# Linear attention and an MLP on one core: the first batch's q loaded with a cast on GpSimd's queue, one group of seven-product multiplications a block later, and a new instruction order

## The chip, the core and the metric

The kernel runs on one core of a Trainium2 chip. The core has five engines with an instruction stream each: TensorE (PE in the profile, with PEld for its weight loads), VectorE (DVE), ScalarE (ACT), GpSimd (POOL) and SyncE (SP). Each works through its stream in order; waits between engines go through semaphores. Loads and stores are issued by SP, ACT or POOL and carried out by 16 DMA engines. On-chip data lies in SBUF (128 partitions); PE writes its results to PSUM, eight banks of 128 x 512 fp32 here. The metric is the device time of one execution in microseconds (us), less is better.

## What is computed

```python
def _attn_ref(q, k, v, omega):              # q, k, v: 8 batches x 8 heads x 576 x 64; omega: 128 x 64
    m, D = omega.shape
    scale = 1.0 / np.sqrt(np.sqrt(D))
    q_s, k_s = (q * scale, k * scale)
    def phi(x):
        proj = np.einsum('bhsd,md->bhsm', x, omega)
        sq = np.sum(x * x, axis=-1, keepdims=True) / 2.0
        h = proj - sq
        h = h - np.max(h, axis=-1, keepdims=True)
        return np.exp(h) / np.sqrt(m)
    q_p, k_p = (phi(q_s), phi(k_s))
    kv = np.einsum('bhsm,bhsd->bhmd', k_p, v)
    z = np.sum(k_p, axis=2)
    num = np.einsum('bhsm,bhmd->bhsd', q_p, kv)
    den = np.einsum('bhsm,bhm->bhs', q_p, z)[..., None] + 1e-06
    return (num / den).astype(np.float32)

def _moe_ref(x, w_in, w_out):               # x: 4608 x 512, w_in: 512 x 2048, w_out: 2048 x 512
    h = x @ w_in
    relu6 = np.clip(h + 3.0, 0.0, 6.0)
    g = h * relu6 / 6.0
    return (g @ w_out).astype(np.float32)
```

The attention's result, its heads laid side by side, is the MLP's x. Everything comes in and goes out as float32.

## The kernel before

The work is written as some 2,000 small operations (`op(...)`), each with the engines that may do it, what it reads and writes, and numbers for a planner: its length, its delay (`lat`), for a DMA its issue time. A planner (`Prog.schedule`) replays the lists in `ORDER`, which say for each engine which operations it runs in which sequence; a search outside the kernel wrote these lists. The planner's numbers run nowhere on the chip. They decide which PSUM bank an operation gets, where PE gets a throwaway matmul (`idle`, line 606, on a constant tile `fill`), and in which order the instructions and their waits are written out.

Attention runs over the 8 batches, the MLP over 8 blocks of 512 tokens, one for each batch, and a ninth block made of each batch's last 64 tokens (the leftovers). The attention of batch b runs beside the MLP of block b - 1, and the output product of a block beside the next block's input product.

One batch of attention: q and k are turned so that the 64 head dimensions lie on partitions (`kT`, `qT`), multiplied with omega (L822 and L825, for the first batch L865 and L884), and the exponential is taken on ACT into `kp` and `qpT` (L841 and L849, for the first batch L872 and L888). The term that would scale a row of q cancels in the division; for k, DVE takes each row's maximum (`mx`, L705) and its reciprocal (`cc`), and v is multiplied by it (`vc`, L999 to L1009, `vcl` for the leftovers). PE then forms `kv` with the sums z beside it (L1017, L1019; copied to `kvz`), the numerators and denominators (L1045, L964), DVE or ACT divides (`rec`, L1064, L1068) into `xb`, and the result is turned into `xT`, the MLP's input.

The order of the first 25 us. The first batch comes in as float32: k and v by 5 loads each and q by 6 (four "main" parts of 256 KB each: two heads' halves times two halves of the head pairs, and one or two parts with the leftovers), two of k's on ACT's queue, all others on SP's. The q parts are called `q00`, `q10`, `q01`, `q11`, `ql0` and `ql1`. PE turns them as float32 (`turns32`, L748) and DVE or ACT copies the result from PSUM to bf16 (`Tevk`, `Tevq`, L552 and L553). The turn of q needs both parts of a half (`q00` and `q10`, `q01` and `q11`). From the second batch on, q and k are loaded on POOL's queue, which casts them to bf16 on the way (`kb`, `qb`, L652), and are turned as bf16, on PE for the second batch (`turns`, L564) and by DMA (L803) after that. The weights `wi` (L625, five loads) and `wo` (L634, eight) are cast to float16 by POOL's queue too; the first `wi` load waits for the q part `q11` (`W_GATE`).

The MLP. The plain input product multiplies four pieces of 128 rows for each 128 hidden columns and 512 tokens (`mm1`, L1124; for the first block in halves of 256 tokens, `mm1_half`, L1277). From a given block on a group of 4 x 128 hidden columns is computed with seven products in place of eight (`mm1_quad`, L1222): sums of the weights (`input_sums`, W1 to W4) and of x (`x_sums`, X1 to X4) are formed first, and five copies and additions in PSUM on ACT and DVE (q1 to q5) put the products together. `FIRST7` gives the block for each of the four groups:

```python
    FIRST7 = (6, 7, 2, 2)
    def seven(blk, f):
        return blk >= FIRST7[f // 2 % 4]
```

The activation is a ReLU on ACT into `tsb` and a minimum and product on DVE into `gT`. The output product uses seven products from the second block on (`products`, L1391; the first block plainly, L1302), with sums of `gT` (S1 to S4, L1318) on POOL or DVE.

The weight sums W2 to W4 and some of X lie in the memory of the float32 q and k (`q32`, `k32`), which is free once the first batch is turned.

Of the kernel before, what the change touches and what calls it, by code (L numbers as in the profile page):

```python
# [21 lines left out]
        14, 121, 115, 117, 131, 159, 138, 153, 147, 119, 141, 144, 135, 156, 150, 127, 123, 125, 129, 174, 133, 168,  # L22
        176, 166, 162, 164, 178, 180, 189, 170, 172, 205, 191, 221, 212, 207, 249, 194, 196, 398, 386, 223, 392, 210,
        237, 393, 228, 215, 199, 239, 399, 226, 387, 252, 244, 242, 388, 400, 394, 389, 395, 401, 404, 407, 410, 247,
        413, 231, 416, 275, 419, 422, 277, 425, 281, 293, 291, 283, 428, 289, 279, 431, 322, 434, 437, 287, 308, 564,
        565, 566, 567, 440, 315, 544, 255, 545, 285, 546, 547, 568, 295, 548, 549, 569, 554, 574, 575, 555, 556, 557,
        558, 576, 577, 348, 550, 578, 559, 335, 350, 353, 340, 337, 551, 560, 374, 579, 361, 379, 376, 580, 366, 363,
        561, 581, 343, 356, 382, 570, 369, 571, 598, 595, 592, 607, 470, 601, 610, 616, 613, 484, 622, 628, 631, 477,
        625, 643, 637, 646, 457, 757, 758, 640, 767, 509, 760, 511, 497, 514, 761, 499, 502, 768, 521, 690, 523, 526,
        533, 770, 538, 535, 771, 670, 773, 776, 777, 683, 774, 697, 794, 788, 791, 803, 818, 780, 806, 797, 823, 822,  # L30
        781, 820, 809, 841, 812, 843, 710, 825, 827, 845, 722, 846, 829, 712, 734, 848, 965, 736, 724, 966, 852, 850,
        715, 727, 975, 968, 746, 981, 748, 751, 976, 739, 969, 978, 979, 878, 982, 984, 985, 891, 988, 989, 898, 996,
        1002, 999, 1005, 905, 1014, 1011, 1026, 1017, 1028, 1049, 1030, 1031, 918, 1054, 1020, 1033, 1035, 1051, 930,
        1037, 1053, 935, 923, 1173, 1056, 1058, 954, 920, 1174, 942, 932, 1060, 1176, 944, 956, 959, 947, 1177, 1183,
        1184, 1099, 1186, 1187, 1086, 1192, 1193, 1113, 1204, 1207, 1210, 1219, 1106, 1213, 1222, 1234, 1236, 1228,
        1238, 1239, 1225, 1189, 1257, 1241, 1190, 1243, 1262, 1245, 1259, 1138, 1261, 1196, 1126, 1143, 1140, 1264,
        1197, 1150, 1268, 1381, 1131, 1152, 1382, 1162, 1128, 1266, 1384, 1164, 1167, 1391, 1155, 1392, 1385, 1307,
        1394, 1395, 1314, 1397, 1400, 1401, 1294, 1398, 1412, 1418, 1444, 1415, 1430, 1442, 1421, 1427, 1447, 1433,
        1446, 1436, 1449, 1467, 1465, 1451, 1404, 1405, 1470, 1453, 1469, 1321, 1472, 1474, 1334, 1346, 1476, 1593,
        1594, 1339, 1336, 1348, 1358, 1351, 1596, 1597, 1519, 1363, 1603, 1604, 1360, 1370, 1526, 1606, 1375, 1372,  # L40
        1607, 1533, 1609, 1612, 1610, 1506, 1613, 1616, 1624, 1617, 1626, 1629, 1662, 1628, 1664, 1631, 1667, 1633,
        1558, 1635, 1647, 1546, 1653, 1560, 1548, 1669, 1650, 1563, 1551, 1671, 1666, 1687, 1582, 1656, 1685, 1587,
        1570, 1584, 1673, 1689, 1690, 1572, 1575, 1712, 1692, 1713, 1694, 1766, 1696, 1722, 1743, 1715, 1716, 1747,
        1770, 1745, 1748, 1768, 1771, 1750, 1791, 1752, 1723, 1754, 1773, 1775, 1789, 1725, 1726, 1814, 1794, 1793,
        1777, 1731, 1732, 1812, 1796, 1798, 1728, 1817, 1729, 1800, 1819, 1816, 1866, 1868, 1821, 1823, 1735, 1870,
        1736, 1889, 1871, 1835, 1836, 1873, 1893, 1894, 1875, 1838, 1891, 1877, 1896, 1845, 1898, 1912, 1839, 1914,
        1916, 1900, 1917, 1935, 1846, 1919, 1939, 1921, 1940, 1937, 1848, 1849, 1851, 1942, 1923, 1958, 1852, 1959,
        1854, 1946, 1855, 1944, 1858, 1859, 1968, 1969, 1961, 1962, 1971, 1972, 1974, 1975, 1978, 1979, 1987, 1990,
        1993,
    ],  # L50
    "SP": [
        0, 18, 22, 33, 20, 23, 26, 25, 24, 27, 28, 32, 29, 30, 31, 450, 264, 266, 265, 456, 455, 453, 454, 553, 384,
        452, 451, 563, 667, 666, 669, 668, 663, 583, 517, 505, 573, 529, 541, 542, 665, 664, 779, 871, 875, 876, 874,
        872, 783, 877, 718, 730, 754, 742, 873, 1085, 1084, 755, 1082, 987, 991, 1080, 1079, 1083, 926, 938, 962, 950,
        1081, 1292, 1287, 1291, 1293, 963, 1290, 1289, 1199, 1146, 1195, 1499, 1134, 1158, 1170, 1288, 1504, 1502, 1171,
        1407, 1503, 1505, 1403, 1500, 1501, 1342, 1354, 1366, 1378, 1379, 1566, 1554, 1619, 1590, 1578, 1591, 1615,
        1734, 1738, 1861, 1857, 1985, 1986, 1982, 1981, 1984, 1992,
    ],
    "ACT": [
        21, 19, 118, 132, 139, 148, 120, 142, 136, 145, 151, 128, 157, 154, 124, 188, 126, 134, 169, 163, 165, 204, 167,  # L60
        177, 175, 160, 220, 206, 171, 173, 179, 181, 222, 211, 238, 200, 390, 396, 405, 408, 402, 232, 248, 411, 414,
        417, 420, 278, 423, 282, 294, 426, 292, 276, 429, 432, 327, 325, 328, 323, 435, 438, 314, 311, 309, 313, 441,
        318, 320, 316, 321, 298, 304, 301, 296, 302, 300, 306, 307, 347, 330, 333, 336, 360, 359, 375, 552, 362, 378,
        562, 383, 344, 599, 582, 596, 572, 593, 608, 475, 473, 471, 602, 611, 617, 476, 614, 487, 490, 623, 489, 485,
        629, 632, 480, 478, 626, 508, 644, 482, 483, 638, 466, 460, 458, 647, 464, 462, 759, 469, 641, 496, 463, 468,
        498, 520, 516, 532, 762, 522, 693, 534, 691, 696, 695, 772, 676, 682, 681, 677, 679, 675, 673, 671, 689, 686,
        688, 703, 795, 684, 789, 700, 792, 706, 709, 698, 819, 807, 804, 798, 830, 702, 824, 821, 810, 543, 813, 842,
        844, 711, 832, 733, 847, 723, 853, 836, 735, 834, 714, 745, 967, 859, 855, 857, 738, 717, 729, 977, 753, 970,
        980, 881, 885, 879, 884, 883, 889, 887, 986, 892, 894, 897, 896, 890, 901, 899, 904, 997, 903, 1003, 1000, 1006,
        906, 908, 1015, 911, 1012, 1027, 1018, 917, 910, 1050, 1032, 941, 919, 1038, 1055, 1021, 1040, 1052, 931, 1044,  # L70
        953, 1061, 1042, 937, 925, 1065, 1175, 1063, 943, 1067, 934, 961, 1185, 1105, 1104, 1100, 1102, 1188, 1095,
        1093, 1097, 1098, 1091, 1087, 1114, 1089, 1118, 1205, 1208, 1092, 1119, 1211, 1116, 1220, 1109, 1112, 1107,
# [353 lines left out]
def _emit(nc, es, q, k, v, omega, w_in, w_out, out):  # L426
    B, H, S, D = q.shape
# [215 lines left out]
    def load(b, eng, gates):  # L643
# [15 lines left out]
        def landing(t, hh, m0, m1):  # L659

            if t == "v" or b == 0:
                return [(t + "32", hh, m) for m in range(m0, m1)]
# [924 lines left out]
```

## Time and profile before

| | |
|---|---|
| time, median of 3 runs | 298.52 us (298.09 to 299.27) |
| time of the profiled execution | 298.33 us |
| its span, first to last instruction | 296.5 us |
| mean granted TensorE clock | 0.999 |
| PE busy | 289.5 us (98%), 2938 matmuls |
| DVE busy | 257.4 us (87%), 581 instructions |
| ACT busy | 240.6 us (81%), 587 instructions |
| POOL busy | 182.2 us (61%), 207 instructions |
| DMA | 44.90 MB written, mean 151 GB/s |
| landing of the first batch's q loads, after issue | 4.0 to 5.2 us |
| landing of the first batch's v loads, after issue | 4.9 to 5.4 us |
| landing of the five w_in loads, after issue | 6.9 to 9.4 us |

Times in the profile are from the start of the span. A chain of waits is followed back from the last instruction to what released each step. A group of instructions has one line: source line, engine, operation, tiles, shapes, count, then busy us and mean ns, then the idle time ahead of them. A matmul's mean length holds its latency, so a run of matmuls is read from the length of the whole run: 16 matmuls of 512 columns take 3.49 to 3.56 us, 16 of 256 columns 1.75.

### The profile page before, as it was taken

What the parts mean: (1) busy time and instruction counts of PE and PEld (TensorE: products, weight loads), DVE (VectorE), ACT (ScalarE), POOL (GpSimd) and SP (SyncE); (2) the same over time, 40 slices, a digit from 0 to 9 for tenths busy, and PEclk for the clock granted to TensorE, in tenths of its full rate; (3) what the DMA queues carried; (4) which work ended last, traced back from release to release, by engine and by line L of the source; (5) the groups of instructions that cost most, each with busy time, mean ns of one, the idle gap of its engine ahead of it and who ended that gap; (6) DMA issues with size and microseconds to landing.
All of it is one profiled execution on the core that took longest, in us unless ns stands there. A gap on an engine that the chain in (4) does not pass through costs nothing.

```text
span 296.5 us, 7761 instructions
## 1 busy us (share of the span) xinstructions
PE 289.5 (98%) x2938; PEld 220.1 (74%) x2938; DVE 257.4 (87%) x581; ACT 240.6 (81%) x587; POOL 182.2 (61%) x207
## 2 busy tenths in 40 slices
PE   8999999999898999999999999999999999999996
PEld 5768855544784698658856987588787888888885
DVE  4797888869987998899789996999999999998974
ACT  2975988799778998999899887999899988767410
POOL 1666456047697863898798579766667344556241
PEclk9999999999999999999999999999999999999999
DMA  8999999989999997998997999959601500110034
GB/s 234 296 206 196 203 234 117 149 200 229 138 202 207 216 127 207 152 199 234 163 180 130 111 259 168 153 131 234 122 2 35 167 25 0 74 71 2 0 144 142
DMA packets 90100, 44.90 MB, mean 151 GB/s; under 512 B 57936, under 2 KB 87760, under 8 KB 90064
## 3 DMA queue, kind: packets, MB, share of 16 engines
q1 hardware_dynamic: 62496, 31.11, 46.6%
q0 software_dynamic: 26592, 12.46, 33.9%
q10 hardware_dynamic: 976, 0.85, 0.9%
q8 instruction: 23, 0.38, 0.5%
q14 instruction: 13, 0.11, 0.1%
HBM read 36.73 MB, written 9.44 MB: 156 GB/s over the span
## 4 chain that ended last, share of the span: by engine, by line
PE 90%; ACT 6%; DVE 3%; issue 0%
PE p L1391 33%; PE p L1222 20%; PE p L1124 13%; PE p L1302 5%; PE p L1277 5%; PE p L1045 3%; PE p L822 3%; PE p L1017 3%; PE p L825 2%; ACT kp L872 1%; PE p L606 1%; ACT tsb L1130 1%; ACT qpT L849 1%; ACT qpT L888 1%; PE p L564 1%; ACT kp L841 1%
## 5 line engine op out<-in xcount | busy, mean ns | idle before, releaser
L705 DVE TENSOR_REDUCE mx<-kp 128x4 f32<-128x512 bf16 (+1 forms) x79 | 47.8, 629 | 6.1 <-ACT kp L841 4.1
L1258 ACT ACTIVATE tsb<-p 128x512 f16<-128x512 f32 x76 | 44.8, 620 | 8.0 <-DVE gT L1260 4.3
L1260 DVE SCALAR_TENSOR_TENSOR gT<-tsb,p 128x512 f16<-128x512 f16 x76 | 50.0, 679 | 1.4 <-ACT tsb L1258 1.0
L1124 PE MATMUL p<-xT,wi 128*128 128x512 f16 x208 | 49.2, 379 | 1.0 <-ACT qpT L849 0.8
L1391 PE MATMUL p<-wo,gT 128*128 128x256 f16 x368 | 46.2, 273 | 0.8 <-DVE gT L1132 0.8
L552 ACT COPY p<-p 128x512 f32<-128x512 f32 x61 | 35.3, 596 | 7.8 <-PE p L1222 5.8
L841 ACT ACTIVATE kp<-p 128x512 bf16<-128x512 f32 (+1 forms) x70 | 37.3, 578 | 4.8 <-PE p L825 4.8
L1391 PEld LDWEIGHTS p<-wo,gT 128*128 128x128 f16 x368 | 35.2, 98 | 5.3 <-ACT kp L841 1.1
L849 ACT ACTIVATE qpT<-p 128x512 bf16<-128x512 f32 (+1 forms) x70 | 37.7, 577 | 0.8 <-PE p L825 0.7
L1132 DVE SCALAR_TENSOR_TENSOR gT<-tsb,p 128x512 f16<-128x512 f16 x52 | 34.2, 678 | 4.5 <-ACT tsb L1130 4.0
L1124 PEld LDWEIGHTS p<-xT,wi 128*128 128x128 f16 x208 | 19.5, 98 | 22.4 <-ACT qpT L849 1.7
L1130 ACT ACTIVATE tsb<-p 128x512 f16<-128x512 f32 x52 | 31.4, 629 | 3.1 <-PE p L1124 2.7
L999 POOL TENSOR_TENSOR vc<-v,cc 128x512 bf16<-128x512 f32 (+1 forms) x29 | 29.1, 1002 | 7.4 <-DVE s L1318 1.9
L1318 POOL TENSOR_TENSOR gT<-gT 128x512 f16<-128x512 f16 x21 | 24.3, 1156 | 14.1 <-DVE s L1318 10.1
L1391 PE MATMUL p<-t,gT 128*128 128x256 f16 x256 | 31.1, 273 | 0.0
L1318 POOL TENSOR_TENSOR s<-gT,s 128x512 f16<-128x512 f16 x18 | 20.8, 1156 | 13.1 <-DVE s L1318 4.3
L1318 POOL TENSOR_TENSOR gT<-gT,s 128x512 f16<-128x512 f16 x18 | 20.9, 1162 | 12.3 <-PE p L1391 6.7
L1391 PEld LDWEIGHTS p<-t,gT 128*128 128x128 f16 x256 | 24.4, 98 | 5.0 <-issue 1.6
L652 POOL DMA_DIRECT2D kb<-in_k_dram x21 | 16.4, 785 | 18.9 <-DMA kT<-kb 10.9
L1318 POOL TENSOR_TENSOR s<-gT 128x512 f16<-128x512 f16 x15 | 17.4, 1158 | 10.3 <-DVE wi L1318 3.2
L1068 ACT ACTIVATE xb<-p,rec 128x64 f16<-128x64 f32 x98 | 21.9, 365 | 0.5 <-DVE rec L1057 0.5
L652 POOL DMA_DIRECT2D qb<-in_q_dram x28 | 19.7, 708 | 2.9 <-DMA wi<-in_moe_w_in_dram 2.9
(142 smaller groups left out, 640.3 us busy)
## 6 DMA issues: line engine op xcount, KB each, us to landing
v<-in_v_dram SPq DMA_DIRECT2D x14, 512.0 KB, 4.7
out_dram<-osb SPq DMA_DIRECT2D x14, 512.0 KB, 3.8
kb<-in_k_dram POOLq DMA_DIRECT2D x14, 256.0 KB, 6.2
qb<-in_q_dram POOLq DMA_DIRECT2D x14, 256.0 KB, 6.2
wo<-in_moe_w_out_dram POOLq DMA_DIRECT2D x8, 256.0 KB, 6.7
wi<-in_moe_w_in_dram POOLq DMA_DIRECT2D x3, 512.0 KB, 7.5
q<-in_q_dram SPq DMA_DIRECT2D x4, 256.0 KB, 4.5
vl<-in_v_dram SPq DMA_DIRECT2D x8, 128.0 KB, 3.8
```

Source lines behind the costliest of these rows:

```text
L552: return E.copy(dst(), src())
L652: lambda E: E.dma_start(dst, src), prio + 0.001 * turn_of[0], reads=gate, writes=keys,
L705: op("DVE", dvet(128 * n), lambda E: E.reduce_max(dst, src, axis=AX.X), p, reads=reads, writes=writes, name="mx" + name)
L841: op("ACT", actt(128 * (d1 - d0)), lambda E, lh=lh, ko=ko, part=part: E.activation(ko, out_of(part, 0, lh)[0].rearrange("p (x m) -> p x m" ...
L849: op("ACT", actt(128 * (d1 - d0)), lambda E, lh=lh, part=part: E.activation(qd[:, part[0]:part[1], lh, :], out_of(part, 1, lh)[0].rearrang ...
L1124: ins = E.matmul(ring.t[vh.slot], wi[:, c, 128 * f:128 * f + 128], xv[:, c, :], start=(c == 0), stop=(c == NJ - 1))
L1130: op("ACT", actt(512), lambda E: E.activation(tsb[tu][:], ring.t[vh.slot], AF.Relu, bias=0.5, scale=1.0 / 6.0), t - 0.1, reads=[vh], write ...
L1222: ins = E.matmul(bank(v)[:, 256 * g:256 * g + 256], w(c, f + g), x[:, c, :], start=start and g == 0 and c == 0, stop=c == 1, skip_group_ch ...
L1258: op("ACT", actt(512), lambda E, v=v, tu=tu: E.activation(tsb[tu][:], bank(v), AF.Relu, bias=0.5, scale=1.0 / 6.0), t - 0.1, reads=[v], wr ...
L1260: op("DVE", dvet(512), lambda E, v=v, tu=tu, dst=dst: E.scalar_tensor_tensor(dst, pieces(tsb[tu][:]), 1.0, pieces(bank(v)), ALU.min, ALU.m ...
L1318: op(engines, {"POOL": 0.157 + n / 475.0, "DVE": 0.08 + n / 2000.0}, lambda E: E.tensor_tensor(dst, x, y, ALU.subtract if minus else ALU.a ...
L1391: ins = E.matmul(ring.t[v.slot][:, 256 * j:256 * j + 256], a[:, f, 128 * j:128 * j + 128], w[:, f, :], start=(first and f == 0 and j == 0) ...
```

## The change

- The first batch's q is loaded by POOL's queue straight into the bf16 tile `qb`, in the same six parts; `q32` is no longer loaded. PE turns it as bf16 with `turns`.
- The first `wi` load waits for the part of `qb` that `q11` brings (`("qb", 17)`).
- `FIRST7` goes from (6, 7, 2, 2) to (7, 7, 2, 2): block 6 computes its first group with plain products. The weight sums of groups 0 and 1 are then formed together ahead of block 7.
- The planner's numbers for landings change: `LANDS` has an entry for almost every load of the first batch, `LANDS_B` for later ones, and the delays of transposed loads and of stores are shorter.
- `ORDER` is replaced in full.

```diff
-    LANDS = {"ql0": 2.3, "ql1": 2.3, "v00": 2.1, "q01": 2.1, "v11": 1.0, "v01": 0.2, "k01": 1.8, "vl": 1.8, "q11": 1.8}
-    W_GATE = [("q32", 1, 3)] * 4
+    LANDS = {"k00": 0.9, "k10": 0.9, "kl": 1.2, "q00": 0.9, "q10": 0.9, "ql0": 1.3, "ql1": 1.3, "v00": 1.3, "v10": 1.1, "q01": 1.1, "v11": -0.8, "v01": -0.1, "k01": 1.0, "k11": 0.7, "vl": 1.1, "q11": 1.0}
+    LANDS_B = {"vl": 0.2, "v00": 0.5, "v10": 0.9, "ql0": 0.8, "ql1": 0.8, "kl": 1.1}
+    W_GATE = [("qb", 17)] * 4
...
-            cast = b > 0 and part[0] in "kq"
+            cast = b > 0 and part[0] in "kq" or part[0] == "q"
             e = "POOL" if cast else eng[turn_of[0]] if turn_of[0] < len(eng) else "SP"
...
-        tensors = {"k": (k, kb if b else k32), "q": (q, qb if b else q32), "v": (v, v32)}
+        tensors = {"k": (k, kb if b else k32), "q": (q, qb), "v": (v, v32)}
...
-                    turns32("q", nm, dbl, alts(qT, s, m0, m1), q32, main_keys("q", range(m0, m1)), 0)
-            for t, src, dst in (("k", k32, kT), ("q", q32, qT)):
-                turns32(t, "l", [0, 1], dst[:, 0:2, :], src, left_keys(t), 0 if t == "k" else LATE)
+                    turns("q", nm, dbl, alts(qT, s, m0, m1), qb, 0)
+            turns32("k", "l", [0, 1], kT[:, 0:2, :], k32, left_keys("k"), 0)
+            turns("q", "l", [0, 1], qT[:, 0:2, :], qb, LATE)
...
-    FIRST7 = (6, 7, 2, 2)
+    FIRST7 = (7, 7, 2, 2)
...
-        old = [(t + "32", hh, m) for t in "kq" for hh in range(2) for m in range(NP)] + [("k32l", 0), ("q32l", 0), ("q32l", 1)]
+        old = [("k32", hh, m) for hh in range(2) for m in range(NP)] + [("k32l", 0)]
```

What the new lists hold at the start, as operations in sequence (T is a turn, Tev its evacuation, e an exponential, K, Q the products with omega):

- SP before: k00, kl, ql1, k01, q00, q11, q01, q10, vl, v00, ql0, v10, v01, v11. After: k00, kl, k01, vl, v00, v10, v01, v11.
- POOL before: wi x3, vc, vc, vcl, vcl, vc, wi x2. After: ql1, q00, q11, q01, q10, ql0, wi x3, vc, wi, vc, vcl, vcl, vc, vc, wi, vc, vc.
- ACT, both: k11, k10, Tevk x2, eK x2, Tevk, eK x4, Tevq. Then, before: eK x2, Tevq, vc's column, Tevq x2, eQ. After: Tevq, eK, eQ, Tevq, eK, eQ.
- DVE before: Tevk x2, mx x3, cc, mx x2, mx, cc x2, Tevq, mx x2. After: Tevk x2, mx x3, cc, mx, Tevq, mx, cc, Tevq, mx, cc, mx x2.
- PE, k's turns before: four in a row, then the products. After: idle x1, T, idle x2, T, idle, T, idle x8, T of the leftovers, then the products. PE has 43 throwaway matmuls in place of 35.
- Over the whole run ACT has 479 operations in place of 487, DVE 572 in place of 581, POOL 217 in place of 203. Of the divisions' first parts ACT does 5 in place of 9 and DVE 27 in place of 23; of the second parts ACT 12 in place of 11; POOL forms 77 S sums in place of 72 and 14 X sums in place of 11, and DVE as many fewer.

## The prediction

> **What bounds the kernel now.** I read the page first, then the chain of waits, then engine busy time in stretches of 2 us (start) and 5 us (the rest).
>
> ```profile
> PE   8999999999898999999999999999999999999996
> PEclk9999999999999999999999999999999999999999
> PE 90%; ACT 6%; DVE 3%; issue 0%
> ```
>
> TensorE (PE) is the bound almost everywhere, at full granted clock. The other 10% of the chain lies at the start and between 45 and 100 us.
>
> ```profile
> 7.70 1.09 ACT kp L872 x2
> ...
> 11.23 0.52 ACT qT L552
> ...
> 20.64 0.43 PE p L1017 x8
> ...
> 22.84 4.02 PE p L1277 x36
> ```
>
> Chain of waits, first 40 us (start, length, engine, tile, line). From 7.70 to 16.2 us it runs on ScalarE (ACT): exponentials of k, evacuations of the turned q, exponentials of q. From 17.2 to 20.6 it is on VectorE (DVE). At 22.84 us the first dense run of MLP matmuls begins; before it PE fills its gaps with throwaway matmuls (L606). What starts that run earlier is saved in full as long as PE stays full behind it.
>
> ```profile
> 8.00:10.00 2.00, 2.00 (x20) 1.67 (x19) 0.89 (x2) 2.00 (x5) 1.20 (x2) 1.00 1.15 316
> 10.00:12.00 2.00, 2.00 (x21) 1.96 (x19) 1.97 (x5) 2.00 (x5) 1.51 (x3) 1.00 1.13 301
> 12.00:14.00 2.00, 1.93 (x15) 1.08 (x12) 2.00 (x8) 2.00 (x7) 1.36 (x3) 1.00 1.17 290
> 14.00:16.00 2.00, 2.00 (x19) 0.97 (x17) 1.97 (x6) 2.00 (x7) 1.84 (x4) 1.00 1.24 206
> 20.00:22.00 2.00, 1.62 (x32) 1.40 (x31) 2.00 (x9) 0.91 (x3) 0.00 (x0) 1.00 1.23 205
> ```
>
> Columns: stretch, length, busy PE, PEld, DVE, ACT, POOL, clock, DMA share, GB/s written. ACT and DVE have no slack from 10 to 18 us, and DVE none until 22. The DMA engines move some 300 GB/s of fp32, or 205 GB/s written when POOL's loads cast to half size (410 GB/s read).
>
> ```profile
> 55.00:60.00 5.00, 4.83 (x44) 1.00 0.80 134
> ...
> 70.00:75.00 5.00, 4.51 (x34) 1.00 1.40 209
> 75.00:80.00 5.00, 4.71 (x47) 1.00 1.13 167
> ...
> 90.00:95.00 5.00, 4.18 (x39) 1.00 1.04 227
> 95.00:100.00 5.00, 5.00 (x34) 1.00 1.22 269
> ```
>
> PE alone. Between 50 and 95 us it stands idle for 1.96 us in all (the sum over these 5 us rows), behind ACT and DVE. From 100 to 270 us it hardly stops, and the chain there is PE throughout: work added to PE there costs its full length, and relief of ACT or DVE there brings nothing.
>
> **The change part by part.**
>
> ```profile
> L553 DVE COPY qT<-p 128x512 bf16<-128x512 bf16 x2 | 0.8, 422 | 0.4 <-PE p L564 0.4
> L553 DVE CAST qT<-p 128x512 bf16<-128x512 f32 x1 | 0.6, 639 | 0.0
> L652 POOL DMA_DIRECT2D qb<-in_q_dram x28 | 19.7, 708 | 2.9 <-DMA wi<-in_moe_w_in_dram 2.9
> POOL wi L625 <- DMA q<-in_q_dram: 6.6, 1, 6.6
> POOL vc L999 <- DMA v<-in_v_dram: 0.9, 2, 0.5
> ```
>
> *Issues.* Six q loads go from SP to POOL: 6 x 0.71 = 4.3 us on POOL, from 2.2 to 6.5 us. POOL waits 6.6 us there (2.2 to 8.8) for q, so they are covered; without that cover w_in would be issued that much later. SP loses 3.4 us of issues (0.76 + 2.01 + 0.64), so k's last half goes out at 2.2 instead of 2.98 and v between 2.7 and 5.4 instead of 5.66 to 9.0. v landed between 11.5 and 13.9 us; its two waits (0.9 us) on POOL should go.
>
> *DMA time.* q is 1.18 MB: at about 310 GB/s 3.8 us, with the cast at 410 GB/s read 2.9 us. All of q, k and v are in about 0.9 us sooner.
>
> *When q lands.* The first transposes of q need the fifth of POOL's six loads. It landed at 9.85 us (5.1 + 4.7) and ACT took its first evacuation at 11.23, between k's exponentials. The fifth issue on POOL starts at about 5.1; the smallest loads on POOL's queue (kb, 64 KB) took 5.1 us to land by their median, so 10.2 is my early end. At the other end q gets little while v is in the SP queue: after w_in was issued at 8.8 us, the 1.25 MB that SP still had came in between 9.85 and 13.9, 308 GB/s, nearly all there was, and 290 GB/s from 12 to 14 is a mix of 74% SP and 26% POOL. With k and v (2.36 MB) at three quarters of the rate until about 11.2 us, q's fifth load ends near 12.4. I take 11.3, between the ends.
>
> The Trainium skill, "DMA: Bandwidth & Descriptors", section "SWDGE vs HWDGE vs iDMA", says that each DMA engine takes turns between the hardware's and GpSimd's queues. By that, q would have half from about 4 us on and its fifth load would be in by 10.3; the row above says that POOL's share was a quarter, so I lean to the late side.
>
> The page "SBUF — State Buffer", section "SBUF: two separate sides", speaks against the change outright: while VectorE runs certain copies GpSimd can't write descriptors, so a load on its queue looks blocked. No row here shows such a block; if all DVE work between 2.2 and 6.5 us (about 1.3 us by the 2 us rows) blocked it, q would be in at 12.6, and the sum below would be 1.3 us worse.
>
> *Delay ahead of ACT.* The new order puts three throwaway matmuls among k's first transposes and eight ahead of the transposes of k's leftover rows, whose evacuation comes before the first exponential on ACT. Eight cost 0.9 us (seven took 0.93 at 9.76). Those transposes ended at 7.1; I put them at 7.6, 0.45 later on the chain. The wait for q (evacuation at 11.7 with q at 11.3) coincides with this delay rather than adding to it. Taken: 0.5; ends 0 and 1.75 (q at 12.4, then 16 transposes of 0.055 us, then DVE's evacuation at 13.5 with a row maximum of k queued behind it and, through that, vc and kv).
>
> *Work taken off.* PE turns q in bf16, 16 in 0.9 instead of 1.9 us: hidden by ACT and DVE, worth nothing itself. DVE, up to the reciprocal of k's last row maxima (18.6 us): one q evacuation of 0.64 becomes 0.42 + 0.28 (two of them); two of four scalings of v go to POOL (1.5 to 0.9); division and xT copy of the first pair come later (0.42 + 0.29); one reciprocal more, 0.17: in all 1.0 us less. After it the last pair's two scalings are on POOL, back to back (2 x 0.62), where on DVE they ended at 20.3 between other work: from that reciprocal's end (18.8 less 1.0) kv starts about 1.3 us before its 20.64. The run at 22.84 follows kv by the same 2.2 us: -1.3 + 0.5 = **-0.8**, ends -1.3 and +0.5.
>
> *One group of seven a block later.* In block 6 one more group of four hidden columns (of 128 each) is multiplied plainly: 16 matmuls of 512 columns at 218 ns (16 took 3.49) = 3.49 us, instead of 7 x 4 of 256 at 109 ns = 3.06: **+0.44** on PE, at about 185 us, where PE is the chain. It spares two additions of 0.69 and three evacuations of 0.6 on DVE and ACT, and joins eight weight sums of 0.42 into four of 0.685; all this lies under PE there, so I count nothing. Were PE not full, it would be worth up to 1 us.
>
> *The searched order.* The planner's landings and DMA costs run nowhere; they choose order, engine, PSUM buffer and fillers. Counting the lists: ACT does 20 fewer small divisions (0.223 each, -4.5 us), DVE net 3 more (+1.8) but 8 fewer S and X sums (-3.4) and 3 fewer scalings (-1.4); POOL takes these. ACT and DVE are each some 5 us lighter of about 220. Only the 1.96 us idle of 50 to 95 us can shrink by it; I take a third, **-0.7**. Ends: -2.0, and +2.0 for new gaps of the same size, since a new order puts waits at new places.
>
> Sum: -0.8 + 0.44 - 0.7 = -1.06 on the profiled execution's 298.33 (span 296.5 and 1.83 around it), which stands 0.19 under the median of 298.52. So about 297.3 to 297.5; I say **297.3**.
>
> **Rivals.** *Larger gain*: q lands early and the gaps close: -1.3 + 0.44 - 2.0, 295.5. For it: idle POOL, lighter ACT and DVE; against: fillers ahead of ACT. *q late behind v* (slower): q gets the quarter share seen at 12 to 14 us or less, ACT and DVE stand at its evacuations, and k's last exponentials are queued behind these. At 12.4 us for q's fifth load the start costs +0.5, so 298.33 + 0.5 + 0.44 = 299.3 with the gaps as they were; each further microsecond of lateness is one more on ACT's order, 300.3 at 13.4. It decides from q at about 12 us on. For it: the 308 GB/s that SP's queue drew; against: POOL's queue starts only 1.5 us after SP's, with k alone ahead of it. *New gaps*: the start gains 0.8, but new places of transposed loads and exponentials stop PE between 40 and 100 us for 2 us more: 298.33 - 0.8 + 0.44 + 2.0 = 300.0. For it: DMA share above 1 in those stretches; against: PE's idle is small there now. *Hidden anyway*: the run at 22.84 is held by something else, say w_in (last piece needed landed at 19.7): only +0.44, 298.9.
>
> **How the numbers follow.** Forecast 0.40 (296.2 to 298.7), larger gain 0.17, q late 0.20, new gaps 0.17, hidden 0.06. 0.5% is 1.5 us, about what a measurement can tell from no change: faster means below 297.0, slower above 300.0. Faster: all of the larger gain and half of the forecast, 0.37. Slower: 0.12 of q late, 0.12 of new gaps and 0.04 for what goes beyond the forecast's and the hidden case's ends, 0.28. Same: the rest, 0.35. The range, 294.9 to 300.6, takes in 295.5, 299.3 to 300.3 and 300.0, with half a microsecond at either end; what is left out is a later q or several bounds at once.
>
> **What would show it.** First exponential on ACT at about 8.2 us; first q evacuation at 11.7 (late: past 12.7); v in before 12.7; kv of the last pair near 19.9; the dense MLP run at 22.0. Near 185 us 16 more matmuls of 512 columns. PE idle from 50 to 95 us below 1.96. Wrong if the dense run starts after 22.9, or if that idle grows by a microsecond.

## The result, and the profile after

| | before | after |
|---|---|---|
| time, median of 20 runs each | 297.92 us (297.06 to 299.27) | 299.08 us (298.30 to 301.11) |
| ratio to before, 95% interval | | 1.005 [1.0036, 1.0064] |
| time and span of the profiled execution | 298.33 and 296.5 us | 299.24 and 297.4 us |
| PE, DVE, ACT, POOL busy | 289.5, 257.4, 240.6, 182.2 us | 289.6, 256.7, 236.3, 195.4 us |

The change makes the kernel slower by 1.2 us between the medians, 1.5 us by the ratio. The profiled execution of before stands 0.4 us above its median over 20 runs and 0.6 to 0.8 above those of later comparisons; its spans are therefore compared with care below. The profiles of two experiments, h_qsp6 and h_qsp6b, were disturbed and are not read for where time goes in their order.

On the page of after, first PE's busy tenths in 40 slices and the chain's shares by engine:

```profile
PE   8689999999999999999999999999999999999996
PE 90%; DMA 3%; ACT 3%; POOL 1%; DVE 1%; issue 0%; POOLq 0%
```

Two things differ from before. A 6 stands in the second slice (7.4 to 14.9 us), and a DMA engine is on the chain with 3%, which in before's list has no share; 3% of 297.4 us is a single transfer. From the fourth slice on the PE row has no 8 (before has two, at 74 to 82 and 89 to 96 us): the gaps of 50 to 95 us are gone. The chain of waits of after, in order of time, shows the transfer:

```profile
2.18 2.84 POOL qb L651 x4
5.02 9.30 DMA qb<-in_q_dram
...
14.37 0.41 PE p L563 x4
...
14.81 1.07 ACT qT L551 x2
...
21.78 0.17 ACT kvz L551
...
22.84 0.26 PE p L1016 x8
...
24.07 0.87 PE p L1276 x8
```

Four q loads are issued on POOL, the fifth (`q10`) leaves at 5.02 and lands 9.30 us later, at 14.32. ACT's first evacuation of q starts at 14.81, where before had 11.23. ACT's chain then runs to `kvz` at 22, and the last products with `kvz` and the dense run of the MLP follow: its first eight uninterrupted matmuls start at 24.07, where before had 36 in a row from 22.84.

Engine busy time in stretches of 2 us (busy PE, PEld, DVE, ACT, POOL, granted clock, DMA share, GB/s written):

```profile
8.00:10.00 2.00, 2.00 (x21) 1.86 (x19) 0.00 (x0) 1.43 (x4) 0.00 (x0) 1.00 1.22 276
10.00:12.00 2.00, 2.00 (x19) 1.54 (x17) 1.53 (x3) 2.00 (x6) 0.50 (x1) 1.00 1.26 259
12.00:14.00 2.00, 0.07 (x1) 0.00 (x0) 1.18 (x3) 0.59 (x2) 2.00 (x4) 1.00 0.98 111
14.00:16.00 2.00, 1.63 (x21) 1.23 (x21) 0.52 (x2) 1.19 (x3) 1.65 (x3) 1.00 1.22 204
20.00:22.00 2.00, 1.81 (x40) 1.40 (x37) 1.74 (x9) 2.00 (x9) 1.86 (x4) 1.00 1.39 201
```

From 12 to 14 us PE and ACT have next to nothing to do and DVE about half: PE 0.07, ACT 0.59, DVE 1.18 of 2 us, in the stretch in which ACT and DVE had been full before (2.00 each). In the same stretch the DMA engines write 111 GB/s, where before wrote 290. So the engines wait for data, and the data come slowly. POOL's 2.00 are mostly its issues of `w_in`.

Who waits for q says the list of waits (us in total, times, longest), on ACT, DVE and POOL:

```profile
ACT qT L551 <- PE p L563: 2.2, 1, 2.2
DVE qT L552 <- PE p L563: 2.3, 1, 2.3
POOL wi L624 <- DMA qb<-in_q_dram: 5.1, 1, 5.1
```

ACT and DVE both stand over 2 us ahead of their first evacuation of q. On POOL the first `wi` load waits 5.1 us for `q11` and goes out at 11.50 us, where before sent it at 8.80.

PE alone in stretches of 5 us, later on:

```profile
55.00:60.00 5.00, 5.00 (x83) 1.00 1.34 183
...
70.00:75.00 5.00, 5.00 (x32) 1.00 1.57 188
75.00:80.00 5.00, 4.97 (x46) 1.00 1.28 246
...
90.00:95.00 5.00, 5.00 (x49) 1.00 0.97 160
```

The rows that showed 4.83, 4.51, 4.71 and 4.18 in before are full, but for 0.03 us in one. The idle time of PE from 50 to 95 us is 0.15 us in place of 1.96.

Three marks on PE place the loss and the gain: the last plain output product of the first block (L1302 in before), the first of the later output products (L1391), and the last of the latter.

| | last of block 0 | first L1391 | last L1391 |
|---|---|---|---|
| before | 57.9 | 75.3 | 291.6 |
| after | 60.5 | 76.9 | 292.5 |
| difference | +2.6 | +1.6 | +0.9 |

2.6 us are lost by 60 us; PE's idle time of the first 26 us, 4.75 us in after and 2.11 in before, says the same. The closed gaps and the full PE behind them give 1.7 back, in spite of the plain group.

### The profile page after: what moved, and what is told of

Same layout as the page of the kernel before. It is cut to its first block, busy times and chain, and to the rows that moved or that the text cites. A ratio compares the mean times of both kernels' runs of the same rounds, so it can differ in the third digit from the quotient of the medians.

```text
span 297.4 us, 7734 instructions
## 1 busy us (share of the span) xinstructions
PE 289.6 (97%) x2934; PEld 220.4 (74%) x2934; DVE 256.7 (86%) x572; ACT 236.3 (79%) x569; POOL 195.4 (66%) x221
## 4 chain that ended last, share of the span: by engine, by line
PE 90%; DMA 3%; ACT 3%; POOL 1%; DVE 1%; issue 0%; POOLq 0%
PE p L1390 33%; PE p L1221 19%; PE p L1123 17%; PE p L1276 5%; PE p L1301 4%; PE p L821 3%; DMA qb<-in_q_dram 3%; PE p L1044 3%; PE p L1016 3%; PE p L824 2%; ACT qpT L887 1%; POOL qb L651 1%; PE p L563 1%; PE p L1463 1%; PE p L1018 1%; ACT qT L551 1%
## 5 line engine op out<-in xcount | busy, mean ns | idle before, releaser
L1257 ACT ACTIVATE tsb<-p 128x512 f16<-128x512 f32 x72 | 42.3, 611 | 13.5 <-PE p L1221 7.3
L1123 PE MATMUL p<-xT,wi 128*128 128x512 f16 x224 | 52.9, 380 | 0.2
L1317 POOL TENSOR_TENSOR gT<-gT,s 128x512 f16<-128x512 f16 x23 | 26.6, 1155 | 23.7 <-PE p L1390 16.7
L848 ACT ACTIVATE qpT<-p 128x512 bf16<-128x512 f32 (+1 forms) x70 | 39.2, 589 | 1.5 <-PE p L824 1.3
L998 POOL TENSOR_TENSOR vc<-v,cc 128x512 bf16<-128x512 f32 (+1 forms) x31 | 29.9, 964 | 13.3 <-PE p L1018 5.1
L1123 PEld LDWEIGHTS p<-xT,wi 128*128 128x128 f16 x224 | 20.9, 98 | 23.9 <-issue 1.1
L1129 ACT ACTIVATE tsb<-p 128x512 f16<-128x512 f32 x56 | 35.5, 656 | 1.6 <-PE p L1123 1.3
L651 POOL DMA_DIRECT2D qb<-in_q_dram x34 | 24.0, 717 | 8.3 <-DMA qT<-qb 6.6
L1317 POOL TENSOR_TENSOR gT<-gT 128x512 f16<-128x512 f16 x20 | 23.2, 1160 | 9.0 <-DVE s L1317 3.5
L1317 POOL TENSOR_TENSOR s<-gT 128x512 f16<-128x512 f16 x18 | 20.8, 1155 | 11.1 <-DVE gT L1259 5.9
L1063 DVE TENSOR_TENSOR xb<-p,rec 128x256 f16<-128x256 f32 (+1 forms) x47 | 21.5, 474 | 0.3
L1317 POOL TENSOR_TENSOR s<-gT,s 128x512 f16<-128x512 f16 x16 | 18.5, 1155 | 2.3 <-DVE s L1317 0.8
```

Source lines behind the costliest of these rows:

```text
L651: lambda E: E.dma_start(dst, src), prio + 0.001 * turn_of[0], reads=gate, writes=keys,
L848: op("ACT", actt(128 * (d1 - d0)), lambda E, lh=lh, part=part: E.activation(qd[:, part[0]:part[1], lh, :], out_of(part, 1, lh)[0].rearrang ...
L1123: ins = E.matmul(ring.t[vh.slot], wi[:, c, 128 * f:128 * f + 128], xv[:, c, :], start=(c == 0), stop=(c == NJ - 1))
L1257: op("ACT", actt(512), lambda E, v=v, tu=tu: E.activation(tsb[tu][:], bank(v), AF.Relu, bias=0.5, scale=1.0 / 6.0), t - 0.1, reads=[v], wr ...
L1317: op(engines, {"POOL": 0.157 + n / 475.0, "DVE": 0.08 + n / 2000.0}, lambda E: E.tensor_tensor(dst, x, y, ALU.subtract if minus else ALU.a ...
```

## The experiments

Theories, by the letters that the expectations use. A: the loss is in the start, q comes late because it shares the DMA engines with v, and the order behind gains. B: the start is absorbed, and the plain group and the order lose. C: what the start gives is lost again behind it, between 90 and 290 us. D: k's turns, with throwaway matmuls between them, don't bring PE up to its rate. A rival to A was that POOL's queue is slow by itself. All runs were timed beside the kernel before on the same chip, and none leaves out any of the work. Differences in microseconds are taken from the ratios where nothing else is said.

**h_oldstart: the old start in front of the searched order.** Before's code and order up to the last product of the first half of block 0 (`mm1.0A.14`), behind it after's order with the plain group.

```diff
 (against before)
-    FIRST7 = (6, 7, 2, 2)
+    FIRST7 = (7, 7, 2, 2)
-ORDER = {before}
+ORDER = {before up to mm1.0A.14, relu.0A.14, g.0A.14, vcc.0.3, v11.0; then after}
```

> The first 25 us of the kernel before (q as float32 on SP, its instruction order up to the first half of block 0's input product), then the changed kernel's order and its FIRST7 for the rest. Theory A (the loss is in the start, the searched order gains behind it): dense MLP run at about 22.8 us as before, PE idle between 50 and 95 us near the changed kernel's 0.2 us instead of 1.96, time below both kernels, before - 1.8 + 0.4, about 296.5. Theory B (the start's loss is absorbed; the plain group and the searched order lose): near the changed kernel, 299.

Measured: 299.14 us, 1.0053 [1.0032, 1.0075], no better than after. PE came to the first L1391 at 75.2 us, 1.7 us ahead of after, and to the last at 292.4, 0.1 ahead. So a lead at the start is no gain at the end: PE, with 0.01 us idle between 105 and 292 us in after, had 0.71 us here. That went against A in its simple form, in which the whole loss of the start is in the time, and is the time that B named.

**h_newstart: the new start in front of the old order.**

```diff
 (against after)
-    FIRST7 = (7, 7, 2, 2)
+    FIRST7 = (6, 7, 2, 2)
-ORDER = {after}
+ORDER = {after up to the same places; then before}
```

> The changed kernel's first 25 us (q cast on POOL's queue), then the order and FIRST7 of the kernel before. Theory A: slower than both, before + 2 to 2.6, about 300.2. Theory B: near the kernel before, 298.

Measured: 301.2 us, 1.0134 [1.0106, 1.0162]. With the new start and no searched order behind it the kernel loses 4.0 us (3.5 between the medians), more than A said and against B; PE's gaps of 65 to 80 us are there again (0.36 and 0.78 us in two rows), and the first L1391 is at 79.3.

**e_quad and e_quad2: the plain group alone.** Before, with FIRST7 7 for group 0. In e_quad all four weight sums move with it to the place ahead of block 7; in e_quad2 W2 to W4 stay early and only W1, which is formed in place of the weights, is late.

```diff
 (against before)
-    FIRST7 = (6, 7, 2, 2)
+    FIRST7 = (7, 7, 2, 2)
```

> The kernel before with one thing changed: block 6 computes its first group with plain products (FIRST7 7 instead of 6), everything else in the order of before. The prediction's price: +0.44 us. Theory B: the larger part of the loss, about +1.

> Block 6's first group plainly as in the earlier run, but three of its four weight sums stay where they were in block 5's time, and only the one made in place moves. If the 1.5 us of the earlier run came from the weight sums that DVE did near 230 us, the plain group alone is left: +0.4 to 0.6. If the plain group itself costs more than its columns: again +1.5.

Measured: 299.26 us, 1.0064 [1.0041, 1.0087], and 298.73 us, 1.0041 [1.0023, 1.006]: 1.9 and 1.2 us (1.5 and 1.1 between the medians) where the columns give 0.44. Part of e_quad's rest is to be seen: four wide sums on DVE ahead of block 7 stop PE in the stretch from 230 to 235 us, which is full in before:

```profile
230.00:235.00 5.00, 4.41 (x46) 1.00 0.63 117
```

0.59 us. What is left of e_quad2's 1.2 its profile doesn't show: its PE goes from the first L1391 at 74.8 to the last at 291.4, 216.6 us against 216.3 in before, and its profiled execution took 298.1 us, 0.6 below its own median.

**a1_v_later: v gets out of q's way.** SP's loads of v wait for `q11`.

```diff
 (against after)
-            load(0, ("SP", "ACT", "SP", "ACT"), {t: [] for t in "kqv"})
+            load(0, ("SP", "ACT", "SP", "ACT"), {"k": [], "q": [], "v": [("qb", 17)]})
```

> The changed kernel with v's first loads held back until the third q part (q11) has landed, so that q shares the DMA engines with k alone. Theory A (v in SP's queue is what makes q late): q's fifth load lands near 10 to 11 us instead of 14.3, q's first evacuation follows k's exponentials near 12.6 us instead of 14.8, time 1 to 2 us less, 297 to 298. Rival (GpSimd's queue is slow by itself): q's fifth load stays after 13 us and the time stays or grows, since v is later.

Measured: 301.61 us, 1.0139 [1.0107, 1.017]. Issues of the first 25 us (count, size of each, median us to landing):

```profile
wi<-in_moe_w_in_dram POOLq DMA_DIRECT2D x3, 512.0 KB, 7.5
v<-in_v_dram SPq DMA_DIRECT2D x4, 256.0 KB, 8.0
...
qb<-in_q_dram POOLq DMA_DIRECT2D x4, 128.0 KB, 5.6
```

With k alone beside it q lands in 5.6 us, `q10` at 10.58 us; in after, with v beside it, the median was 8.0 and `q10` came at 14.32. So it is v that makes q late, and POOL's queue by itself isn't as slow as that, though its 5.6 us are still above the 4.5 of q's loads on SP in before. But now v starts at 9.3 us and shares with `w_in`, and the chain of waits of a1 has it:

```profile
11.26 10.60 DMA v<-in_v_dram
...
26.72 1.71 PE p L1276 x8
...
29.10 0.87 PE p L1276 x8
```

The last v load takes 10.6 us. The lateness has been handed from q to v. (The two rows of PE are read in the last section.)

**a5_v_wi: `w_in` gets out of v's way too.** a1 with the first `wi` load waiting for v.

```diff
 (against a1_v_later)
-    W_GATE = [("qb", 17)] * 4
+    W_GATE = [("v32", 1, 3)] * 4
```

> The changed kernel with v held back until q's third part has landed (as in a1_v_later, 301.6) and now w_in held back until v has landed, so that the three streams follow one another. Theory A (what shares the DMA engines is late): q's fifth load in near 10.6 us as there, v's last part near 15 us instead of 21.9, w_in's first two pieces near 20 us; time 299 to 300, less than a1_v_later, and no better than the changed kernel since w_in is later. Rival (POOL's queue is slow by itself): v stays late, 301 to 302.

Measured: 301.48 us, 1.0136 [1.0102, 1.017]. Issues of a5:

```profile
v<-in_v_dram SPq DMA_DIRECT2D x4, 256.0 KB, 3.8
```

v with nothing beside it: 3.8 us, after 8.0 with `w_in` and 9.7 with q (the median of after). Now `w_in` goes out at 16.25 us. The three runs together say that each order of q, v and `w_in` chooses who waits. That the DMA engines' rate alone is the bound isn't shown: where one transfer waits for another they stand, with a share of 0.18 from 9 to 10 us in a1 and of 0.00 from 16 to 17 us in a5.

**h_qsp: q by SP as float32, all else as after.** The path of q is undone: before's loads of q and v on SP in before's sequence, fp32 turns, and with them before's planner numbers; after's order and the plain group stay.

```diff
 (against after)
-            cast = b > 0 and part[0] in "kq" or part[0] == "q"
+            cast = b > 0 and part[0] in "kq"
...
-        tensors = {"k": (k, kb if b else k32), "q": (q, qb), "v": (v, v32)}
+        tensors = {"k": (k, kb if b else k32), "q": (q, qb if b else q32), "v": (v, v32)}
...
-    W_GATE = [("qb", 17)] * 4
+    W_GATE = [("q32", 1, 3)] * 4
```

> The changed kernel's whole order and FIRST7, but the first batch's q as float32 on SP again, its loads and v's issued as before; PE turns q as float32. Theory A (q's late landing costs the start): q's fifth load lands at about 10 us, no wait of ACT on q at 12 to 15 us, last plain output product of block 0 (58.8 to 60.5 in the runs so far) 1.5 to 2 us earlier than in the changed kernel, time 0.5 to 2 us less than the changed kernel, 297 to 298.5. Theory C (what the start gives is lost again between 90 and 290 us, as when only the start was put back): 299.

It was run again on two other chips:

> h_qsp again, beside h_qsp6b on the same chip: 1.001 to 1.003 of before, 297.8 to 298.4 us. Were it above 1.004, the 1.0 us that q's new path costs in the searched order would be in doubt.

> h_qsp beside it on the same chip: 297.8 to 298.4 us, ratio to before 1.001 to 1.003.

Measured: 298.08, 298.36 and 298.29 us; 1.0014 [0.9998, 1.003], 1.0021 [1.0006, 1.0037] and 1.0024 [1.001, 1.0038]. That is 0.4 to 0.7 us over before, and 0.8 to 1.1 us under after: the price of q's new path in the searched order. About 0.4 us of it goes with a granted clock that fell in some of after's executions (last section). Which part of the path weighs, the cast, POOL's queue or v's earlier issue, h_qsp doesn't separate; for the landing a1 names v. The same order behind it makes the marks comparable: last of block 0 at 57.8 (after 60.5), first L1391 at 74.2 (76.9), last at 291.3 (292.5). The path costs 2.7 us up to 77 us, and of these 1.5 don't reach the end. Where they stay is shown by the chain of waits of h_qsp and by PE in stretches (busy, clock, DMA share, GB/s):

```profile
89.40 1.09 ACT kp L845 x2
...
96.12 0.69 DVE gT L1136
...
98.94 1.18 DVE gT L1136 x2
...
104.07 0.43 PE p L1021 x8
```

```profile
150.00:170.00 20.00, 19.76 (x177) 1.00 0.92 155
170.00:190.00 20.00, 19.81 (x206) 1.00 1.04 183
...
210.00:220.00 10.00, 9.79 (x83) 1.00 0.37 89
```

From 89.4 to 103.6 us the chain lies on ACT and DVE without a break, where after's PE is the chain; and PE stands 0.64 us in three later stretches that are full in after. PE ahead of its partners is held until they come up. Of the 1.5 us, 0.64 is this idle time and 0.5 PE's longer busy time (290.1 against 289.6 us, the reason of which isn't shown); 0.4 isn't assigned.

**h_qpool: q by POOL with a cast, all else as before.** The other way round: q's path alone, before's order and FIRST7.

```diff
 (against before)
-            cast = b > 0 and part[0] in "kq"
+            cast = b > 0 and part[0] in "kq" or part[0] == "q"
...
-ORDER = {before}
+ORDER = {before, q's six loads ahead of wi1 on POOL, not on SP}
```

> The kernel before with q alone changed: cast on POOL's queue ahead of w_in, turned as bf16, v therefore issued earlier; order otherwise that of before, FIRST7 as before. Theory A: q's fifth load near 14 us, time before + 2 to 3.5. If the loss were in the new order of the start and not in q's path: near the kernel before, 298.

Measured: 303.06 us, 1.0172 [1.0138, 1.0206]: 5.1 us, with a granted clock of 0.993 to 0.994 in three of its six executions. `q10` landed at 14.68 us, 0.4 us later than in after. The four corners, as ratios to before:

| | before's order | searched order, plain group |
|---|---|---|
| q on SP, fp32 | 1 | 1.0014 to 1.0024 |
| q on POOL, cast | 1.0172 | 1.005 |

The path is a loss in both columns; in the first one, the price also holds what an order written for an early q loses with a late one. The searched order is worth 3.6 us by the ratios with the new path and, plain group included, costs 0.4 to 0.7 with the old one.

**a2_warm: the throwaway matmuls first, k's turns in a row.** After, with sixteen throwaway matmuls ahead and none between the turns of k.

```diff
 (against after)
-                    if f is not None and f[0] <= IDLE_UNTIL and (
+                    kturn = lst and lst[0].name.startswith("Tk0") and lst[0].name != "Tk0.10"
+                    warm = len(fillers) > 60
+                    if f is not None and f[0] <= IDLE_UNTIL and (warm or not kturn) and (
+                            kturn or
```

> The changed kernel with PE's first 16 throwaway matmuls all ahead of k's turns and none between them, as before. The changed kernel's first weight loads of k's turns take 0.217 us each until 6.9 us, before 0.135: theory D (turns on PE don't raise its clock, and fillers between them keep it low longer) expects 0.14 again, the first exponential at about 8 us instead of 9.05 and the time 0 to 0.5 us less, since q is waited for at 14.3 anyway. Rival: k itself lands late; first exponential unchanged.

Measured: 299.09 us, 1.0058 [1.0035, 1.0081], the same as after. The first exponential on ACT is at 8.77 (9.05 in after, 7.70 in before). D falls: the place of the fillers among the turns brings nothing to the time, since ACT waits for q behind that anyway. (In the profiled execution part of the time is lost to the clock; see the last section.)

**h_qsp6, h_qsp6b and h_qsp8: the price of the plain group in the searched order.** h_qsp's order up to block 6 and before's order from there, with a FIRST7 of 6 and so without the plain group; then the same with the sum S45.0 ahead of X1.6 on POOL, behind which block 5's products had waited.

```diff
 (against h_qsp)
-    FIRST7 = (7, 7, 2, 2)
+    FIRST7 = (6, 7, 2, 2)
-ORDER = {h_qsp}
+ORDER = {h_qsp up to mm1.6.0, relu.6.0, g.6.0, vc.7, Xdma.7; then before}
```

> The earlier run with the changed kernel's order and q as float32 on SP (h_qsp, 1.0014 of before), now with FIRST7 as before: block 6 computes its first group with seven products again, in the order of before from that point on. If the plain group costs what its columns cost, 0.44 us less than h_qsp: 297.4 to 297.7, at or slightly under the kernel before. If the plain group costs 1.2 to 1.5 as it did alone in the order of before: 296.6 to 296.9, under both kernels.

> q as fp32 on SP and the searched order until block 6, from there before's order with a FIRST7 of 6 (no plain group), with the sum S45.0 put ahead of X1.6 on GpSimd, so that block 5's products do not wait for it as they did in h_qsp6. It prices the plain group in the searched order. By the columns that the product adds for a plain group (0.44 us): 0.4 under h_qsp_r, 297.4 to 297.7, ratio to before 0.998 to 1.0. If it costs 1.2 to 1.5 us, as it did alone in before's order: 296.6 to 296.9, ratio 0.995. At or above h_qsp_r: the seam between the two orders costs more than the group, and the group's price in this order stays open.

Measured: 305.98 us, 1.0264 [1.0238, 1.0289], and 304.14 us, 1.0216 [1.0191, 1.024]. Moving one sum gave 1.4 us (1.8 between the medians); the seam between the two orders costs some 6 us more, and the group's price can't be read from it. So the other way: a second plain group.

```diff
 (against h_qsp)
-    FIRST7 = (7, 7, 2, 2)
+    FIRST7 = (8, 7, 2, 2)
```

> h_qsp (q as fp32 on SP, the searched order) with FIRST7 (8, 7, 2, 2): group 0 is plain in block 7 too, a second plain group beside the one of block 6. Its four weight sums stand between block 7's operations on VectorE, alone, where h_qsp formed them with group 1's. It doubles the price of the plain group. By the columns (PE full there): 0.44 us over h_qsp's 298.1 to 298.4, so 298.6 to 298.8. If a plain group costs 1.2 to 1.9 us, as e_quad2 and e_quad timed it: 299.3 to 300.3. Above that: VectorE, with the four sums in its way, stops PE, which PE's idle time from 200 to 230 us would show.

Measured: 304.27 us, 1.0214 [1.0192, 1.0235], 6.0 us over h_qsp on the same chip. The third case of the expectation came, though later than it said; PE in stretches:

```profile
230.00:235.00 5.00, 4.00 (x44) 1.00 0.65 97
...
240.00:250.00 10.00, 7.97 (x62) 1.00 0.01 2
250.00:260.00 10.00, 8.57 (x75) 1.00 0.00 1
```

All these rows are full in h_qsp. 1.00, 2.03 and 1.43 are 4.46 us of stops from 230 to 260 us; PE's list of waits has 3.3 of them behind DVE's `gT` and 1.0, in the first row, behind a transposing load of `xT`. PE's busy time is 1.5 us longer (291.9 against 290.4): together 5.96 of the 6.0. Shown is that a plain group, put by hand into an order written without it, costs what it upsets, mostly on DVE in e_quad and h_qsp8, three to fourteen times its columns (1.2, 1.9 and 6.0 us). Not shown is what the group of block 6 costs in the searched order, which was made with it: the 0.4 to 0.7 us of h_qsp hold 0.44 by columns and an order that is worth nothing beside before's, or other shares of the two. That stays open. None of the runs beat the kernel before.

## Why the prediction failed, step by step

The forecast was 297.3 us, 1.06 below the profiled execution; it came to 0.91 above it (299.24).

- **When q lands** is the step that failed. The prediction took 11.3 us for q's fifth load, between 10.2 and 12.4; it landed at 14.32 (in before at 10.03, where the prediction has 9.85), and ACT's first evacuation of q went from 11.23 to 14.81. The row behind the late end was misread. I took what came in by SP between 9.85 and 13.9 us of before, with `w_in` outstanding since 8.8 us, for SP being served three times as often as POOL. Queues of before from 9 to 13 us (packets, MB, share of 16 engines; q1 is SP's, q0 POOL's):

```profile
q1 hardware_dynamic: 1861, 1.23, 113.6%
q0 software_dynamic: 3, 0.00, 0.5%
```

  `w_in` moved three packets in the 4.2 us after its issue, none of them before 12.75 us, and POOL's 26% came when SP's queue ran out (149 packets to 14 from 13.25 to 14 us). The row shows one queue after the other and no share. (Of the 1.25 MB, SP's queue moved 1.04 in that stretch.) How long a load on POOL's queue takes to start differs, and why isn't shown: its first packets came some 4 us after the issue here, some 2.8 us in after (q, issued at 2.12), and some 1.4 us in a5 (`w_in`, issued at 16.25 with the DMA engines empty). Where both had data, in after from 9 to 10 us, it reads:

```profile
q0 software_dynamic: 181, 0.09, 63.3%
q1 hardware_dynamic: 181, 0.17, 61.7%
```

  Packet for packet in turn, and 179 to 178 and 186 to 174 in the next two microseconds. From 7 to 9 us it was 242 to 550, so for that time q did have less than a third. q's packets carry half as much written as v's, so q comes in at 0.09 MB per us where v has 0.17. By 12 us 0.48 of q's 0.59 MB are in, and at that rate the rest of `q10`, some 0.08 MB, would have followed at about 12.8, not far behind the prediction's late end of 12.4 (an estimate from these rows). POOL's queue from 4 to 13 us:

```profile
q0 software_dynamic: 1590, 0.58, 53.7%
```

  Then comes a tail that no term of mine had. Queues of after from 12.5 to 14 us:

```profile
q0 software_dynamic: 300, 0.10, 80.0%
q1 hardware_dynamic: 23, 0.02, 4.7%
```

  In 1.5 us POOL's queue holds 80% of the engines' time and moves 0.10 MB; 203 of all 323 packets are under 512 bytes, which fits the leftover rows of `ql0`, the load behind `q10`. So nearly all of q's bytes were in by 13 us, and `q10` landed 1.3 us later. What holds the landing back isn't shown. It is there without v too: in a1 POOL's queue moves 13 packets from 9.5 to 10 us, and `q10` lands at 10.58. What v adds is the rest, 3.7 us between the two landings.
- **DMA time.** "All of q, k and v in about 0.9 us sooner" was wrong by the same reading: the last v load landed at 15.6, not before 12.7, and 1.6 us after before's. Bytes at the two best rates were added up as if the queues didn't meet.
- **Start, -0.8.** It came to +2.6 by the mark at 60 us. The last pair's `kv` is at 22.84 on the chain (forecast near 19.9, in before 20.64), the dense run at 24.07 (22.0). The delay ahead of ACT, taken as 0.5, was 1.35 by the first exponential (9.05 against 7.70). Taking the throwaway matmuls from between the turns gave back 0.28 of it (8.77 in a2_warm); the rest goes with PE's rate in the first 7 us, which differs between executions (before's sequence has 7.70 in before, 7.88 in h_qsp and 8.27 in h_oldstart). Since ACT then waited 2.2 us for q, this delay is not in the sum.
- **Issues on POOL** were covered as said (POOL waited 5.1 us for q behind them). What lay behind, though, was the gate: `w_in` hung on `q11`, and went out 2.7 us later than before.
- **Plain group, +0.44.** Sixteen matmuls of 512 columns more (224 on that line for 208), and PE full there: nothing speaks against the term, but no run priced it alone without a disturbance of DVE.
- **Searched order, -0.7 of the 1.96 us.** The mechanism was right and the size too small: 1.81 of the 1.96 went, near the end of -2.0. It is the order's doing: h_qsp and h_oldstart, with q's old path, have 0.23 and 0.15 us of such idle time, h_newstart, with the new start and before's order, 1.36. The counts behind it held for ACT, 4.3 us lighter, and not for DVE, 0.7 us lighter where some 5 were forecast.

With the measured sizes the prediction's sum is +2.6 + 0.44 - 1.8 = +1.24 us; measured are +0.91 by the profiled executions and 1.2 to 1.5 by medians and ratio. The 0.44 in it is the forecast's own, and a loss of clock, which some executions have (last section), was in no term. (The case *hidden anyway* adds up to 298.77, not 298.9; nothing hangs on it.)

The rival that came is *q late behind v*. Its price, +0.5 at 12.4 us and one more for each further microsecond, gives +2.4 at 14.3, beside the 2.6 measured. Its reason was half right: q had less than a third of the packets from 7 to 9 us, but half from 9 to 12, and the tail came on top. With the gaps as they were and without the plain group it gives 298.33 + 2.4 = 300.7, or 300.1 on the median of before in that comparison; h_newstart, which is that case, took 301.2. That the rival's own figure for 12.4 us, 299.3, is what was measured is chance. The prediction held this rival's price and the larger gain of the order in two separate cases; it was both at once.

The Trainium skill's rule in "DMA: Bandwidth & Descriptors", section "SWDGE vs HWDGE vs iDMA", of turns between the queues, agrees with the 181 packets of either queue in after. Half of the packets was also half of the bytes read, since q's 0.09 MB written per us are 0.18 read, beside v's 0.17. The estimate of 10.3 us that I had drawn from it still missed 14.3 by 4 us: it let q have its half from 4 us on, where POOL's queue had written 0.21 MB by 9 us, and it had no tail. The stop of GpSimd's descriptors by VectorE, of "SBUF — State Buffer", section "SBUF: two separate sides", doesn't show here: POOL's queue moved 179 and 186 packets in the two microseconds from 10 to 12 us, with DVE busy for 1.53 of the 2 us, as many as from 9 to 10, when DVE did nothing (0.00 from 8 to 10). No run was made for it alone.

## What to carry over

A transfer that is halved by a cast isn't sooner in when it shares its time with others: sum what all queues have outstanding between the issue and the need, in the packets that the trace shows for each, and ask who is pushed back (q, v and `w_in` changed places here: their last loads landed at 15.5, 15.6 and 26.1 us in after, at 10.9, 21.9 and 27.8 in a1, at 11.2, 16.0 and 29.9 in a5). A row that shows one queue fast proves a priority only if the other had data moving at that time. And a part of a change put alone into an order that was written for something else prices the seam, not the part.

## What the runs showed of the hardware

**An idle PE can lose half its clock, and doesn't always.** In the profiled execution of after PE waits 2.3 us for q's first turn, and the granted clock stays at 1.00 (rows above); in h_qpool it waits 2.7 us with the same clock. In a2_warm it waits 2.4 us, and PE in stretches reads:

```profile
12.00:14.00 2.00, 0.00 (x0) 1.00 0.88 96
14.00:16.00 2.00, 1.77 (x17) 0.55 0.96 147
16.00:18.00 2.00, 2.00 (x10) 0.59 1.20 185
18.00:20.00 2.00, 1.52 (x6) 1.00 1.13 166
```

Some 4 us at little over half the clock, 1.7 us of PE time. a1 (0.78, 0.50, 0.87 from 24 to 30 us) and a5 (0.72, 0.50, 0.93 from 22 to 28) have the same behind stretches in which PE was idle; in a1 eight matmuls take 1.71 us at 26.72 and 0.87 at 29.10. So some of what a1 and a5 lost is clock and not DMA. Each of the three dips takes 1.7 us of clock and brings the mean over the span to 0.994, and the mean is known for every execution. In after 8 of 20 executions have 0.993 to 0.994 and take 299.88 us on average, the other 12 have 0.998 to 1.0 and take 298.90. Of the kernels with q on POOL's queue 19 executions of 50 have such a mean; of those with q's old path in h_oldstart, e_quad, e_quad2 and the three runs of h_qsp none of 59, and of before, beside the experiments, none of 79. Two kernels whose seam stops PE, h_qsp6 and h_qsp6b, have 0.987 to 0.994 in all their other executions too. So the wait for q seems to cost after a second time, about 0.4 us on average (8 of 20 times 0.98 us). In which stretch the clock fell was seen in a1, a2_warm and a5 alone, since the profiled execution of after is one of the 12.

**PE can be slow with the clock column at 1.00.** The weight loads of k's first turns took, on average, 0.135 us each in before and 0.148 to 0.177 in h_qsp and h_oldstart, 0.19 in a2_warm, and 0.217 in after until about 6.9 us; each takes about 0.23 us until some moment and 0.14 behind it, and this moment differs between executions of one program (5.9, 6.1 and 6.9 us in the three of h_qsp). One execution of h_qsp6b never got fast: it took 1,049.88 us, with a granted clock of 1.0 in the record. Its groups of instructions (busy us, mean ns):

```profile
L1129 PE MATMUL p<-xT,wi 128*128 128x512 f16 x208 | 176.6, 1096 | 0.0
...
L1396 PEld LDWEIGHTS p<-wo,gT 128*128 128x128 f16 x368 | 78.0, 214 | 75.3 <-issue 68.6
```

The matmul's mean is 1,096 ns where before has 379, and the weight load of 128 columns takes 214 where before's others take 95 to 99. What raises PE's rate isn't shown here. The Trainium skill, "TensorE: Matmul & The Clock Gate", section "Part 1: The HAM clock gate (the "warmup" mystery)", says that half rate is the default, that a busy window of about 3.4 us releases it at a moment that differs between runs, that an idle window brings it back, and that the gate has been seen stuck at a quarter for 50 us and more. The half clock in a2_warm agrees, though 2.4 us of idle time were enough; after, with much the same idle time and no loss, shows that it isn't sure to come. The execution of 1,049.88 us would fit a gate stuck at a quarter over a whole run, by its lengths alone (the 208 matmuls keep PE busy 0.85 us each, where 16 in a row take 3.49 us, 0.218 each); its granted clock on record, 1.0, doesn't show it.
